# Attention scores as four 64 x 64 quarters of TensorE instead of full products with a block-diagonal key matrix

## The chip, the cores and the metric

The kernel runs on one core of a Trainium2 chip. The metric is the device time of one execution in microseconds (us), lower is better. Three runs of the kernel before took 565.74, 566.91 and 566.95 us; their median is 566.91 us. One further execution was profiled: it took 566.09 us, of which the span from the first to the last instruction is 564.3 us. The granted TensorE clock in it was 0.998 of full speed.

## The reference

For each of 8 batches, attention with pooled keys and values runs over 8 heads, and a gated MLP with mixing over the tokens follows on its result. All data are float32.

```python
def _attn_ref(q, k, v):                       # q, k, v: (8 batches, 8 heads, 576 tokens, 64)
    pool = 8
    k_p = k.reshape(B, H, 72, pool, D).mean(axis=3)       # 72 pooled keys per head
    v_p = v.reshape(B, H, 72, pool, D).mean(axis=3)
    scores = (1 / sqrt(D)) * np.matmul(q, k_p.transpose(0, 1, 3, 2))     # 576 x 72 per head
    attn = softmax(scores, axis=-1)           # max subtracted, 1e-9 added to the sum
    return np.matmul(attn, v_p)

def _moe_ref(x, w_in, w_spatial, b_spatial, w_out):       # x: (8, 576, 512)
    h = np.maximum(x @ w_in, 0)               # 512 x 1024
    u, v = halves of h
    v_n = (v - mean(v)) / sqrt(var(v) + 1e-6)
    v_s = w_spatial @ v_n + b_spatial         # 576 x 576, mixes the tokens
    return (u * v_s) @ w_out                  # 512 x 512
```

## The kernel before, in words

The work of a batch is cut into named stages. Each stage is a Python generator; every call of `next` records the instructions up to its next `yield`. Three long tables of names, `FIRST` (batch 0 with the loading of the weights), `STEP` (six times, batches 1 to 6) and `LAST` (batch 7), give the order in which the stages are stepped (`run`, line 852). Each engine executes its own instructions in exactly this recorded order, so the tables are the schedule, on TensorE (PE), VectorE (DVE), ScalarE (ACT), GpSimd (POOL) and the DMA queue of SyncE (SP). A name with a capital letter is an attention stage, which runs one batch ahead of the MLP stages in small letters; `+` and `-` move a name by a batch, and the marks `~ ^ ! %` choose a variant of a stage.

Attention stages, per batch; `g` is a pair of heads (0 to 3), `j` a pair of such pairs (0, 1):

- `K`, `V`: load keys and values, sum them in groups of 8. The plain variant does it on DVE (lines 316 to 325), one with a mark on POOL, and the `^` variant on PE, by products with the identity (`pool_pe`, line 331).
- `KT` (`att_keys_t`, line 373): transposes the pooled keys on PE and copies them from PSUM into `kp_bd`. For each pair of heads `kp_bd` holds a 128 x 144 matrix: rows 0 to 63 and columns 0 to 71 for the even head, rows 64 to 127 and columns 72 to 143 for the odd head, and zeros elsewhere, which one memset writes at the start (line 161). Copies go one head of the pair at a time.
- `Q{g}`: brings the queries of two heads into `qT`, 128 rows (2 heads x 64) by 512 tokens, and the last 64 tokens into `pt_q`.
- `S{g}` (`att_softmax`, line 524): the scores of 512 tokens for two heads. Four matmuls, one for each 128 tokens; the 128 x 128 stationary side is `qT`, the moving side the 144 columns of `kp_bd`. They go to `s_ps`, two PSUM banks of which there is one buffer only. The softmax (line 493) then reads `s_ps`: DVE takes the maximum, and either DVE subtracts it and ACT does one exponential over all (plain), or ACT does one exponential per head with the maximum as a bias (`~`), 8 of them. Only then can the next `S` write `s_ps`.
- `U{j}` (`att_softmax_l`, line 535): the same for the last 64 tokens of two pairs of heads. Two matmuls with 64 stationary columns, one into the upper and one into the lower 64 partitions of a buffer from the ring `tp` (`ps_tr`, 3 buffers), and a softmax over 2 heads.
- `T`, `Y`: bring the weights `e` of the softmax into the layout in which `A` needs them (from batch 2 on by DVE transposes and DMAs through DRAM, before that on PE). `A{half}{g}` (`att_av`, line 665): four matmuls per half and pair of heads, the product with the values.

MLP stages: `v` and `u` (products with `w_in`, lines 724, 740 and 767), `s` (product with `w_spatial`, lines 786 to 788, then gating), `o` (product with `w_out`, line 809, then the output). In these, and in `A`, every float32 product is written as three products of a high and a low part in the type float32r. The scores and the pooling are plain float32 products; each of those stands in the trace as two loads of the stationary side (LDWEIGHTS, engine PEld) and two matmuls.

The names `wv`, `wu`, `wo`, `ws` load and split weights into high and low parts. The variant `^` of such a load does the last subtraction on PE, with three products of 512 columns with the identity (lines 252 to 254), the others do it on POOL.

Of the kernel before, what the change touches and what calls it, by code (L numbers as in the profile page):

```python
# [8 lines left out]
F32 = mybir.dt.float32  # L9
# [49 lines left out]
)  # L59
STEP = (  # L60
# [9 lines left out]
)  # L70
LAST = (
# [35 lines left out]
def pooled_attention_gmlp(ctx: ExitStack, tc: tile.TileContext, q, k, v, w_in, w_sp, b_sp, w_out, out):  # L107
    nc = tc.nc
    B, H, S, D = q.shape
    P = 128  # L110
# [262 lines left out]
    def att_keys_t(kp, kr, alt=""):  # L373
# [8 lines left out]
        for e in range(2):  # L382
# [4 lines left out]
            if e == 0:  # L387
                yield
# [501 lines left out]
```

## Time and profile before

| | |
|---|---|
| median of three runs | 566.91 us (565.74 to 566.95) |
| profiled execution | 566.09 us, span 564.3 us |
| PE busy | 549.7 us (97% of the span), 3461 matmuls |
| PEld busy | 493.1 us (87%) |
| DVE busy | 370.3 us (66%) |
| ACT busy | 276.9 us (49%) |
| POOL busy | 258.4 us (46%) |
| DMA | 62.99 MB, 42.0% of the 16 engines' time on the one big queue |

Matmuls overlap in the trace: one that feeds 144 columns is listed with 286 ns, but the next starts 122 ns after it. The time that a matmul costs is therefore read from the chain of waits, where each piece is the time from the end of the piece before it to its own end, or from the distance of starts in the timeline; not from the mean duration in the table of groups.

### The profile page before, as it was taken

What the parts mean: (1) busy time and instruction counts of PE and PEld (TensorE: products, weight loads), DVE (VectorE), ACT (ScalarE), POOL (GpSimd) and SP (SyncE); (2) the same over time, 40 slices, a digit from 0 to 9 for tenths busy, and PEclk for the clock granted to TensorE, in tenths of its full rate; (3) what the DMA queues carried; (4) which work ended last, traced back from release to release, by engine and by line L of the source; (5) the groups of instructions that cost most, each with busy time, mean ns of one, the idle gap of its engine ahead of it and who ended that gap; (6) DMA issues with size and microseconds to landing.
All of it is one profiled execution on the core that took longest, in us unless ns stands there. A gap on an engine that the chain in (4) does not pass through costs nothing.

```text
span 564.3 us, 10082 instructions
## 1 busy us (share of the span) xinstructions
PE 549.7 (97%) x3461; PEld 493.1 (87%) x3461; DVE 370.3 (66%) x901; ACT 276.9 (49%) x806; POOL 258.4 (46%) x357
## 2 busy tenths in 40 slices
PE   4999999999999999999999999999999999999997
PEld 4788799987999889988998889988998889978995
DVE  3677989797857566767867577767867675535110
ACT  2697687653635535363535535363535554433221
POOL 1646565855655144651647133751547154233321
PEclk9999999999999999999999999999999999999999
DMA  8877365458204454257235364255324321100102
GB/s 241 238 231 181 76 139 102 129 140 248 70 19 113 134 108 128 69 156 164 71 98 142 127 132 117 77 148 128 93 76 121 118 76 40 43 20 0 57 2 94
DMA packets 123347, 62.99 MB, mean 112 GB/s; under 512 B 84256, under 2 KB 104736, under 8 KB 123296
## 3 DMA queue, kind: packets, MB, share of 16 engines
q1 hardware_dynamic: 123296, 62.35, 42.0%
q8 instruction: 27, 0.44, 0.3%
q14 instruction: 24, 0.20, 0.1%
HBM read 44.92 MB, written 17.40 MB: 110 GB/s over the span
## 4 chain that ended last, share of the span: by engine, by line
PE 90%; DVE 4%; ACT 3%; DMA 1%; issue 0%; SPq 0%; DVEq 0%; ACTq 0%
PE mm L809 18%; PE mm L786 17%; PE mm L767 17%; PE mm L724 15%; PE s_ps L528 5%; PE mm L331 4%; PE mm L740 3%; PE tp L672 2%; PE mm L788 1%; PE tp L675 1%; PE mm L787 1%; PE tp L673 1%; PE tp L674 1%; DMA st<-in_k 1%; PE tp L539 1%; ACT pt_rr L590 1%
## 5 line engine op out<-in xcount | busy, mean ns | idle before, releaser
L767 PE MATMUL mm<-xT,win_h 128*128 128x256 f32 (+1 forms) x512 | 104.7, 297 | 0.0
L800 POOL TENSOR_TENSOR gT<-g,gT 128x256 fp32r<-128x256 f32 x64 | 49.8, 783 | 87.6 <-ACT gT L797 87.5
L767 PEld LDWEIGHTS mm<-xT,win_h 128*128 128x128 f32 x512 | 82.2, 188 | 2.7 <-issue 1.0
L724 PE MATMUL mm<-win_h,xT 128*128 128x512 f32 x256 | 81.3, 398 | 0.7 <-ACT vv L728 0.7
L809 PE MATMUL mm<-wout_h,gT 128*128 128x512 f32 x256 | 80.7, 396 | 0.0
L786 PE MATMUL mm<-wT_h,vn_h 128*128 128x256 f32 (+1 forms) x256 | 77.2, 302 | 0.0
L786 PE MATMUL mm<-wT_l,vn_h 128*128 128x256 f32 (+1 forms) x256 | 75.8, 296 | 0.0
L786 PE MATMUL mm<-wT_h,vn_l 128*128 128x256 f32 (+1 forms) x256 | 75.7, 296 | 0.0
L767 PE MATMUL mm<-xT,win_l 128*128 128x320 f32 (+1 forms) x256 | 75.1, 293 | 0.0
L521 POOL TENSOR_TENSOR e<-e,rs 128x576 f32<-128x576 f32 (+1 forms) x48 | 44.7, 932 | 59.9 <-DVE rs L519 37.4
L791 DVE TENSOR_TENSOR g<-mm,ru 128x256 f32<-128x256 f32 (+1 forms) x64 | 28.0, 447 | 56.3 <-PE mm L788 53.3
L711 POOL TENSOR_TENSOR rstd<-rstd,neg_half 128x1 f32<-128x1 f32 (+1 forms) x40 | 23.7, 592 | 80.3 <-DVE rstd L709 80.3
L724 PEld LDWEIGHTS mm<-win_h,xT 128*128 128x128 f32 x256 | 47.1, 188 | 11.7 <-ACT vv L728 1.2
L809 PEld LDWEIGHTS mm<-wout_h,gT 128*128 128x128 f32 x256 | 47.3, 188 | 10.4 <-issue 0.2
L734 POOL TENSOR_TENSOR vn_l<-vv,vn_h 128x512 fp32r<-128x512 f32 x32 | 43.2, 1357 | 25.2 <-ACT vn_h L732 19.8
L809 PE MATMUL mm<-wout_l,gT 128*128 128x512 f32 x128 | 50.6, 395 | 0.0
L724 PE MATMUL mm<-win_l,xT 128*128 128x512 f32 x128 | 50.5, 395 | 0.0
L770 ACT ACTIVATE ru<-mm 128x320 f32<-128x320 f32 (+1 forms) x64 | 25.5, 410 | 50.2 <-PE mm L767 50.0
L797 ACT ACTIVATE gT<-g 128x256 fp32r<-128x256 f32 x64 | 26.3, 414 | 46.7 <-DVE g L791 42.1
L786 PEld LDWEIGHTS mm<-wT_h,vn_l 128*128 128x128 f32 x256 | 48.6, 190 | 0.0
L786 PEld LDWEIGHTS mm<-wT_h,vn_h 128*128 128x128 f32 x256 | 48.4, 189 | 0.2
L194 ACT ACTIVATE xT<-tp 128x256 fp32r<-128x256 f32 (+1 forms) x64 | 25.3, 408 | 47.4 <-PE tp L675 47.3
(192 smaller groups left out, 1304.6 us busy)
## 6 DMA issues: line engine op xcount, KB each, us to landing
st<-in_k SPq DMA_DIRECT2D x32, 256.0 KB, 3.3
out<-ob SPq DMA_DIRECT2D x32, 256.0 KB, 2.4
qt<-in_q SPq DMA_DIRECT2D x112, 72.0 KB, 3.2
st<-in_v SPq DMA_DIRECT2D x24, 256.0 KB, 3.4
xd<-X SPq DMA_DIRECT2D x24, 256.0 KB, 2.0
pt_l<-xd SPq DMA_DIRECT2D x24, 256.0 KB, 3.2
stw<-in_moe_w_in SPq DMA_DIRECT2D x8, 512.0 KB, 6.7
st<-in_moe_w_out SPq DMA_DIRECT2D x4, 512.0 KB, 6.6
```

The costliest lines, as they stand in the source:

```text
L194: nc.scalar.activation(hi, src, AF.Copy)
L521: nc.gpsimd.tensor_tensor(em, em, rs.unsqueeze(2).broadcast_to([m, n, SP]), op=ALU.mult)
L528: nc.tensor.matmul(s_ps[:, c // 2, (c % 2) * 2 * SP:(c % 2 + 1) * 2 * SP], lhsT=t["q", g][:, c * P:(c + 1) * P], rhs=kp_bd[:, g, :], start ...
L724: nc.tensor.matmul(a, lhsT=xT[:, i, o + c * P:o + (c + 1) * P], rhs=w[:, i, DH:], start=(i == 0 and j == 0), stop=(i == NK - 1 and j == 2))
L734: nc.gpsimd.tensor_tensor(t["vn_l"][:, c, :], vv, f32(t["vn_h"][:, c, :]), op=ALU.subtract)
L767: nc.tensor.matmul(a, lhsT=w[:, i, d * P:(d + 1) * P], rhs=xT[:, i, o + ts.start:o + ts.stop], start=(i == 0 and j == 0), stop=(i == NK - ...
L770: nc.scalar.activation(t["ru"][:, d, ts], a, AF.Relu)
L786: nc.tensor.matmul(a, lhsT=x[:, c, ds], rhs=y[:, c, ts], start=(c == 0 and j == 0), stop=False)
L791: nc.vector.tensor_tensor(g, a, t["ru"][:, d, ts], op=ALU.mult)
L797: nc.scalar.activation(dst[:, d, 0, at:at + m], g[:, o:o + m], AF.Copy)
L800: nc.gpsimd.tensor_tensor(dst[:, d, 1, at:at + m], g[:, o:o + m], f32(dst[:, d, 0, at:at + m]), op=ALU.subtract)
L809: nc.tensor.matmul(a, lhsT=src[:, i, x, at:at + m], rhs=w[:, i, :], start=(i == 0 and j == 0), stop=(i == ND - 1 and j == 2))
```

## The change

`kp_bd` is replaced by `kT`, which holds for each pair of heads a 128 x 72 matrix: the even head's keys in rows 0 to 63, the odd head's in rows 64 to 127, no zeros. Its memset is gone, and `KT` copies the main part in one instruction over all 128 partitions, then the rest in two.

`S` becomes 16 matmuls of 64 rows (one head) by 64 stationary columns (tokens) with 72 moving columns: for each 128 tokens, two halves of the tokens `i` by two heads `e`. Half `i` writes partitions 64 `i` to 64 `i` + 63, head `e` writes bank `e` of `s_ps`. `U` becomes four such matmuls instead of two, and now writes to `s_ps` and no longer to the ring `tp`. The softmax reads the two banks in the other arrangement, with the same numbers of elements.

The three tables are new. With them some stages take other variants: one more weight load takes the `^` variant (6 instead of 5), more softmaxes take `~` (17 instead of 10 of the `S`, 14 instead of 10 of the `U`), and the pooling of the values in four batches and of a few keys moves from POOL to DVE.

```diff
-    "wv1^ wv1 -K^ wv2~% -K wv2 wv2 -K -K -Q0^ -K -K -K wv1 wo0^ wv1 -Q0 -Q1^ wv1 -KT~ wo0 -Q0 -V^ -KT -Q2^ -V "
...
+    "wv0 wv0 wv0 -K^ wv3~^ -K -K wv3 wv0 -K wv3 wv0 -Q1^ wo1^! -K wv3 -K wv0 -Q0~^ wv3 -K -KT -Q0 wo1 wo1 -KT "
...
-    kp_bd = const.tile([P, NG, 2 * SP], F32, name="kp_bd")
+    kT = const.tile([P, NG, SP], F32, name="kT")
...
-    nc.gpsimd.memset(kp_bd, 0.0)
...
+        copy = nc.vector.tensor_copy if alt else nc.scalar.copy
+        copy(kT[:, :, :KM].rearrange("p (r a) s -> p r a s", r=2), main)
+        yield
         for e in range(2):
             es = slice(e * D, (e + 1) * D)
-            copy = nc.vector.tensor_copy if alt else nc.scalar.copy
-            copy(kp_bd[es, :, e * SP:e * SP + KM].rearrange("p (r a) s -> p r a s", r=2), main[es])
-            copy(kp_bd[es, :, e * SP + KM:(e + 1) * SP], rest[es, :, e, :])
-            if e == 0:
-                yield
+            copy(kT[es, :, KM:], rest[es, :, e, :])
...
         s_ps = ps.tile([P, 2, 512], F32, name="s_ps", tag="s")
+
         for c in range(NC):
-            nc.tensor.matmul(s_ps[:, c // 2, (c % 2) * 2 * SP:(c % 2 + 1) * 2 * SP],
-                             lhsT=t["q", g][:, c * P:(c + 1) * P], rhs=kp_bd[:, g, :], start=True, stop=True)
+            for i in range(2):
+                for e in range(2):
+                    es, at = slice(e * D, (e + 1) * D), c * P + i * TL
+                    nc.tensor.matmul(s_ps[i * TL:(i + 1) * TL, e, c * SP:(c + 1) * SP],
+                                     lhsT=t["q", g][es, at:at + TL], rhs=kT[es, g, :], start=True, stop=True)
         yield
-        em = yield from softmax(s_ps[:, :, :4 * SP].rearrange("p a (h s) -> p a h s", h=4), P, 8, alt)
+        em = yield from softmax(s_ps[:, :, :4 * SP].rearrange("p e (c s) -> p e c s", s=SP), P, 8, alt)
...
-        sl = ps_tr()
+        sl = ps.tile([P, 2, 512], F32, name="s_ps", tag="s")
         for i in range(2):
-            nc.tensor.matmul(sl[i * TL:(i + 1) * TL, :2 * SP], lhsT=t["ql", j][:, i, :], rhs=kp_bd[:, 2 * j + i, :],
-                             start=True, stop=True)
+            for e in range(2):
+                es = slice(e * D, (e + 1) * D)
+                nc.tensor.matmul(sl[i * TL:(i + 1) * TL, e, :SP], lhsT=t["ql", j][es, i, :],
+                                 rhs=kT[es, 2 * j + i, :], start=True, stop=True)
         yield
-        em = yield from softmax(sl[:, :2 * SP].rearrange("p (a h s) -> p a h s", a=1, h=2), P, 2, alt)
+        em = yield from softmax(sl[:, :, :SP].unsqueeze(2), P, 2, alt)
```

The first place at which the new tables matter is PE in the steady part (batches 2 to 7). Before, a `U` stands among the products of `A` (L672 to L675) and writes to the ring `tp`. Lines of the changed kernel are 25 to 29 lower, so that `U` (L539) is L514 there, `S` (L528) is L501, `s` (L786 to L788) is L761 to L763, and `o` (L809) is L784. In the order before:

```order
L809 MATMUL mm<-wout_l,gT 128x512
L672 MATMUL tp<-pt_h,vm_h 128x256
L673 MATMUL tp<-pt_h,vm_l 128x256
L674 MATMUL tp<-pt_l,vm_h 128x256
L675 MATMUL tp<-pt_rr,vr 128x256
L539 MATMUL tp<-kp_bd,pt_q 64x144 x2
L672 MATMUL tp<-pt_h,vm_h 128x256
```

In the order of the change, one `U` and the `S` that follows it, with the 14 products of one `s` between them:

```order
L650 MATMUL tp<-pt_rr,vr 128x320
L514 MATMUL s_ps<-kT,pt_q 64x72 x4
L761 MATMUL mm<-wT_h,vn_h 128x320
...
L762 MATMUL mm<-wT_h,vt 128x320
L763 MATMUL mm<-wT_l,vb 128x320
L501 MATMUL s_ps<-kT,qT 64x72 x16
L784 MATMUL mm<-wout_h,gT 128x512 x2
```

The `U` and the `S` now write the same single buffer `s_ps`, one stage apart. In all other places of the steady part an `S` or a `U` stands alone between full-size products, before and after. On DVE, the maximum of this `U` (L467, L498 before) stands in the order of the change behind a subtraction of the softmax of an `S`, two transposes of `Y` and a product of the gating, which waits for a buffer that POOL frees:

```order
L475 TENSOR_TENSOR e<-s_ps,mx 128x2x4x72
L623 STREAM_TRANSPOSE XL<-e 128x128
L625 STREAM_TRANSPOSE XLR<-pt_p 64x32
L766 TENSOR_TENSOR g<-mm,ru 128x256
L467 TENSOR_REDUCE mx<-s_ps 128x2
L469 TENSOR_SCALAR mx<-mx 128x2
```

The second place is PE at the start. Before, the transposes of queries follow the pooling of the keys, and the first weight split comes behind the transposes of the keys:

```order
L331 MATMUL mm<-st_r,ident 64x64 x8
L474 MATMUL tp<-ident,qt 128x128 x4
L475 MATMUL tp<-ident,qt 128x64
L377 MATMUL tp<-ident,kp 128x128 x2
L378 MATMUL tp<-ident,kr 128x64
L252 MATMUL mm<-x,ident 128x512
L253 MATMUL mm<-win_h,ident_m 128x512
L254 MATMUL mm<-z,ident_p 128x512
```

In the order of the change the first weight split (L223 to L225) stands directly behind the pooling, and the transposes follow:

```order
L302 MATMUL mm<-st_r,ident 64x64 x8
L223 MATMUL mm<-x,ident 128x512
L224 MATMUL mm<-win_h,ident_m 128x512
L225 MATMUL mm<-z,ident_p 128x512
L348 MATMUL tp<-ident,kp 128x128 x2
L349 MATMUL tp<-ident,kr 128x64
L444 MATMUL tp<-ident,qt 128x128 x4
L445 MATMUL tp<-ident,qt 128x64
```

What moved: the split of a weight now covers the time in which ACT copies the pooled keys out of PSUM, which before the first transposes of queries covered.

More of the change, by code (lines that the diff above doesn't have):

```diff
@@ L493, in softmax @@
     def softmax(sv, m, n, alt):
-        a = sv.shape[1]
         mx = ring("mx", 2, [P, 8], F32, "mx")[:m, :n]
-        mv = mx.rearrange("p (a h) -> p a h", a=a)
+        mv = mx.rearrange("p (c e) -> p e c", e=2)
         nc.vector.tensor_reduce(mv, sv, axis=AX.X, op=ALU.max)
@@ L502, in softmax @@
         em = ring("e", 3, [P, 8, SP], F32, "e")[:m, :n, :]
-        ev = em.rearrange("p (a h) s -> p a h s", a=a)
+        ev = em.rearrange("p (c e) s -> p e c s", e=2)
         sm = ring("sm", 2, [P, 8], F32, "sm")[:m, :n]
@@ L513, in softmax @@
             for h in range(n):
-                nc.scalar.activation(em[:, h, :], sv[:, h * a // n, h % (n // a), :],
+                nc.scalar.activation(em[:, h, :], sv[:, h % 2, h // 2, :],
                                      AF.Exp, bias=mx[:, h:h + 1], scale=QK, accum_out=sm[:, h:h + 1])
```

105 rows, old and new, of tables (FIRST, LAST, STEP) are left out of this document.

## The prediction

> **What bounds the kernel now.** I read the page's first part, then the windows over three steady stretches, then what PE waits for.
>
> ```profile
> PE 549.7 (97%) x3461; PEld 493.1 (87%) x3461; DVE 370.3 (66%) x901; ACT 276.9 (49%) x806; POOL 258.4 (46%) x357
> ```
>
> ```profile
> core 0: us, PE busy (x) PEld busy (x) DVE busy (x) ACT busy (x) POOL busy (x), PEclk, DMA share, GB/s
> 0.00:20.00 20.00, 12.16 (x75) 10.26 (x77) 8.32 (x23) 6.60 (x13) 4.91 (x13) 1.00 0.77 218
> 132.00:194.00 62.00, 62.00 (x390) 56.29 (x389) 40.96 (x103) 29.47 (x86) 31.10 (x44) 1.00 0.37 101
> 382.00:447.00 65.00, 65.00 (x404) 58.75 (x403) 48.13 (x120) 31.59 (x92) 28.80 (x43) 1.00 0.39 101
> ```
>
> ```profile
> PE mm L331 <- DMA st<-in_k: 7.8, 1, 7.8
> PE mm L724 <- ACT vv L728: 0.7, 1, 0.7
> PE s_ps L528 <- DVE qT L484: 0.7, 1, 0.7
> PE s_ps L528 <- DVE e L506: 0.6, 1, 0.6
> PE tp L672 <- DVE pt_rr L592: 0.4, 1, 0.4
> PE s_ps L528 <- ACT e L514: 0.2, 1, 0.2
> ```
>
> In a step of one batch PE is busy 62.00 of 62.00 us, while DVE fills 41 to 48, ACT 29 to 32 and POOL 29 to 31. Over the whole span PE waits 7.8 us for the first keys and 2.6 us in five further places. The clock is 1.00, so no throttle hides anything. Hence the time is the sum of what PE's products cost, and the question is what a score group costs between its neighbours, before and after.
>
> **What S and U cost now.** From the chain of waits, where a piece is the time it adds:
>
> ```profile
> 289.13 0.98 PE s_ps L528 x8
> ...
> 308.69 0.12 PE tp L675
> 308.81 0.40 PE tp L539 x4
> 309.20 0.31 PE tp L672
> 309.51 0.12 PE tp L673
> ...
> 41.37 1.07 PE mm L331 x16
> 42.45 0.32 PE tp L672
> 42.76 0.12 PE tp L673
> ```
>
> A full-array S is 8 passes (four products, two passes each) in 0.98 us, 0.122 per pass of 144 columns. A U is 4 passes of 64 stationary columns: it adds 0.40 us, and the first full-size product behind it takes 0.31 instead of 0.12, so it costs 0.40 + 0.19 = 0.59 us. The chain of waits thus shows a price that is paid once for going from the full array to a part of it and back.
>
> How large is it? A U's four passes start at once in pairs, one in the upper and one in the lower column half:
>
> ```profile
> 288.97 1.14 PE L528 MATMUL s_ps<-kp_bd,qT 128*128 128x144 f32 x8
> ...
> 308.73 0.20 PEld L539 LDWEIGHTS tp<-kp_bd,pt_q 128*64 128x64 f32 x4
> 308.74 0.47 PE L539 MATMUL tp<-kp_bd,pt_q 128*64 128x144 f32 x4
> ```
>
> ```profile
> L539 PEld LDWEIGHTS tp<-kp_bd,pt_q x64: 132/134/136, 19.9 to 449.6; 128*64 128x64 f32 x64
> ```
>
> One load of U lasts 0.134 us, yet all four together span 0.20, and the four matmuls, each of median 0.312, span 0.47. Four passes in a row, 0.122 apart, would span 0.312 + 3 × 0.122 = 0.68; two rounds of two span 0.312 + 0.16 = 0.47. So column halves run side by side, U is two rounds, and the round trip costs 0.59 − 2 × 0.122 = 0.346 us. The pooling group on 64 x 64 tiles (16 passes on one and the same quarter) costs 1.07 + 0.20 = 1.27 us; less 0.346 that is 0.92 / 16 = 0.058 per pass of 64 columns.
>
> The Trainium skill has a rule that speaks against this change: "TensorEngine Tiling (Array Packing)", section Key Properties, says that a change of tiling mode drains the array. The trace agrees, with those 0.346 us; by the rule, all 32 S now pay it, 11 us of the 31 that S takes, and this is in the sum below.
>
> **S and U after.** An S becomes 16 products, 32 passes of 72 columns. No row shows four quarters running at once; two column halves are shown above, and two row halves here (two products that read 64 rows each, one from each half, side by side in 0.27 us, where one lasts 272 ns in the groups):
>
> ```profile
> 24.67 0.27 PE L631 MATMUL tp<-ident,e 64*128 64x64 f32 x2
> ...
> L631 PE MATMUL tp<-ident,e 64*128 64x64 f32 x8 | 1.1, 272 | 0.0
> ```
>
> I take it that both hold together, since the order in the code goes through the four quarters one after the other. Then S is 8 rounds. A round of 72 columns costs between half of the 0.122 of 144 columns, 0.061, and 0.058 × 72/64 = 0.065; I take 0.063. S after = 0.346 + 8 × 0.063 = 0.85 us, against 0.98. U after = 0.346 + 2 × 0.063 = 0.47, against 0.59.
>
> - 32 S gain 0.13 each: 4.2 us (0.114 to 0.146: 3.6 to 4.7).
> - 16 U gain 2 × (0.122 − 0.063) = 0.12 each: 1.9 us.
> - Together 6.1 us (5.5 to 6.6).
>
> In the order of the change, as before, nearly every S and U stands alone among full-size products, so no round trip is shared.
>
> **What PE gets in addition.** One more weight load takes the variant that splits on PE:
>
> ```profile
> 16.66 1.06 PE mm L252 x2
> 17.72 0.23 PE mm L253
> 17.95 0.23 PE mm L254
> ```
>
> That is 1.52 us. It stands directly behind the pooling of the keys. Before, PE is through with that pooling at 15.3 us (below), while DVE takes up the first weight piece at 10.63 us and the next at 12.89, so the inputs of the first split are there about 2 us ahead of PE, and I expect no wait. Net on PE: 6.1 − 1.5 = 4.6 us less (4.0 to 5.1).
>
> ```profile
> 10.63 0.43 DVE L226 TENSOR_SCALAR x<-x 128x512 uint32<-128x512 uint32 x1 [7.21 <-ACT x L221]
> 12.89 0.42 DVE L226 TENSOR_SCALAR x<-x 128x512 uint32<-128x512 uint32 x1
> ...
> 15.30 0.59 PE tp L474 x4
> ```
>
> **What I cost at nothing.** Seven more S take the `~` softmax and the pooling of four batches of values goes from POOL to DVE.
>
> ```profile
> 97.11 2.54 ACT e L514 x16
> ...
> L508 ACT ACTIVATE e<-e 128x576 f32<-128x576 f32 x22 | 14.8, 674 | 2.3 <-DVE e L506 2.3
> L506 DVE TENSOR_TENSOR e<-s_ps,mx 128x576 f32<-128x576 f32 x22 | 16.5, 750 | 0.8
> L510 DVE TENSOR_REDUCE sm<-e 128x8 f32<-128x576 f32 x22 | 16.3, 742 | 8.0 <-ACT e L508 8.0
> L320 POOL TENSOR_TENSOR st<-st 128x512 f32<-128x512 f32 x10 | 12.9, 1294 | 0.0
> L320 DVE TENSOR_TENSOR st<-st 128x512 f32<-128x512 f32 x14 | 9.8, 700 | 3.3 <-DMA st<-in_k 3.3
> ```
>
> A `~` adds 2.54 − 0.67 = 1.9 us to ACT and takes 0.75 + 0.74 = 1.5 from DVE. With one or two more in a batch, ACT goes from 31 to at most 35 of 62 us. A pooled piece of values costs DVE 0.70 where it cost POOL 1.29; a batch's worth is 3 to 4 us, about what the `~` take away. DVE stays below 50 of 62, and PE's cover is whole. If it were not, the price is in rival B. The missing memset and the fewer copies of keys lie beside PE's work and count nothing. The five small waits of 2.6 us in all may shift, vanish or grow; the one way in which they vanish reaches 7.2 us gained, and I leave them.
>
> **Sum.** Against the profiled execution: 566.09 − 4.6 = 561.5 us (span 559.7). Against the median of 566.91, 0.8 higher, it is 562.3. I say 562.0, and 561.0 to 562.9 from the bounds of the terms alone; with 2.6 us of waits gained or as much lost, 558.4 to 565.5. A difference of 0.2%, 1.1 us, is the least that counts as one here.
>
> **Rivals.**
>
> *A: only two quarters run at a time.* The trace shows pairs in columns and pairs in rows, never four. If a round holds two, S has 16 rounds: 0.346 + 16 × 0.063 = 1.35 us, 0.37 more than now, 32 × 0.37 = 12 us; U has four rounds, 0.60, no change; with the 1.5 us of the split the time is 566.5 + 13.5 = 580 us. It decides as soon as S needs more than 10 rounds ((0.98 − 0.346) / 0.063). With none together S would be 2.3 us and the time about 612. For it: no row excludes it. Against it: both pairings work on the same loads and matmuls, and the order of the products suits it.
>
> The Trainium skill, "TensorE: Matmul & The Clock Gate", Part 3, "The mechanism", lets a load pass running matmuls only where the row groups differ, by which the two column halves would go one after the other and A would hold. The trace disagrees for two of them, with four loads in 0.20 us, and has no row for four quarters.
>
> *B: the score buffer.* U now writes `s_ps`, of which there is one, and in each of six steps an S follows a U after 14 products of `s`.
>
> ```profile
> 288.98 0.15 PE mm L788
> ...
> 309.25 0.31 DVE L498 TENSOR_REDUCE mx<-tp 128x2 f32<-128x144 f32 x1 [0.55 <-PE tp L539]
> ...
> 270.53 0.47 PE L539 MATMUL tp<-kp_bd,pt_q 128*64 128x144 f32 x4
> 273.47 0.26 DVE L498 TENSOR_REDUCE mx<-tp 128x2 f32<-128x144 f32 x1
> ```
>
> At 0.147 us each, the 14 take 2.06, so S is due 0.47 + 2.06 = 2.5 us after the start of U. With a free DVE the maximum starts 0.51 us after it (308.74 to 309.25), and with 0.31, a scaling of 0.2 and two exponentials of 0.3 the buffer is free after about 1.8 us: no wait. But that maximum stands on DVE behind a subtraction (0.75), two transposes and a gating product that waits for POOL. If it comes 2.94 us after U, as at 270.53, the buffer is free after 4.2 us and PE waits 1.7 us, six times: 10 us, and the whole is 562 + 10 = 572. From 0.8 us of wait a step on it eats the gain. What stands behind that S on PE are the products of `o`, so the time is lost in full. Against it: before, DVE is late by that much in some places only, and PE's other waits on `s_ps` sum up to 1.5 us.
>
> *C: no change.* The round of 72 columns is not shorter than the one of 144, or the new order at the start, where PE is idle for 8 of 20 us, waits for a split or a query by 2 to 4 us more. With S at 0.346 + 8 × 0.08 = 0.99 the gain is gone but for 1.3 us of U, less than the split: 566 to 567.
>
> **How the numbers follow.** The forecast has 0.62 (558.4 to 565.5), A 0.13 (580 or more), B 0.12 (566 to 572), C 0.13 (565 to 568). The time is that of the forecast, 562.0. The range leaves out A and the upper end of B, some 0.17 in all, and takes in the rest: 558.0 to 570.0. Faster by over 0.2% are the forecast and a tenth of B and of C, together 0.65; within 0.2% are most of C and some of B, 0.13; slower are A, the rest of B and of C, 0.22.
>
> **What would show it.** In the changed profile: S (L501) as a piece of 0.60 to 0.70 in the chain of waits and a first product behind it of 0.31; its 32 passes spanning about 0.75 in the timeline, in rounds of four starts; PE at 62 of 62 or less per step, no new row of waits for `s_ps` above 1 us in sum. A piece of 1.1 or more for S means A; a row "s_ps <- ACT" or "<- DVE" of several us means B; a longer wait before 20 us means C. The forecast is wrong if the round trip for four quarters costs more than 0.48, or a round more than 0.08 us, since either takes the gain of S.

## The result

Four runs of the changed kernel took 557.05 us (556.75 to 557.56), the kernel before on the same chip 566.33 (565.66 to 566.95): a ratio of 0.984, 95% interval 0.982 to 0.985. That is 9.3 us faster where 4.6 were forecast, and below the range that was given (558.0 to 570.0).

The page of the changed kernel, first part, then two of the windows and the waits of PE:

```profile
PE 539.7 (97%) x4297; PEld 479.1 (86%) x4297; DVE 374.7 (68%) x930; ACT 291.6 (53%) x916; POOL 229.4 (41%) x316
```

```profile
132.00:194.00 62.00, 62.00 (x523) 55.30 (x525) 39.71 (x100) 31.45 (x102) 29.98 (x42) 1.00 0.43 118
382.00:447.00 65.00, 65.00 (x524) 58.17 (x522) 46.98 (x119) 36.03 (x123) 21.48 (x33) 1.00 0.43 114
```

```profile
PE mm L302 <- DMA st<-in_k: 7.9, 2, 6.6
PE s_ps L514 <- ACT e L483: 1.1, 1, 1.1
PE s_ps L501 <- DVE e L475: 1.0, 1, 1.0
PE s_ps L514 <- DVE e L475: 0.7, 1, 0.7
PE mm L742 <- DVE wT_l L167: 0.4, 1, 0.4
PE tp L552 <- DVE sm L486: 0.3, 1, 0.3
```

PE still fills 62.00 of 62.00 us per step, while DVE, ACT and POOL are below 48 of 62 to 65. The waits for the score buffer, 2.8 us, all fall in the first 34 us; behind them PE waits 0.3 us at 46 us and 0.4 us at 84 us, and then no more. So the kernel is bound as before, and what changed is what PE's products cost. The chain of waits of the changed kernel, an `S` among products of 256 columns and a `U` among products of 320:

```profile
288.74 0.11 PE mm L763
288.85 0.66 PE s_ps L501 x32
289.51 0.32 PE tp L647
289.83 0.11 PE tp L648
...
295.39 0.15 PE tp L650
295.54 0.29 PE s_ps L514 x8
295.83 1.95 PE mm L761 x12
```

`S` costs 0.66 + (0.32 − 0.12) = 0.86 us, where 0.98 stood before and 0.85 was forecast. `U` costs 0.29, and the 12 products behind it 1.95 instead of 12 × 0.147 = 1.76, together 0.48; forecast 0.47, before 0.59. The timeline of an `S` (start, duration, engine, number), and the rows of its line over the whole kernel (least, median and largest ns, first and last start), show the four quarters at work together:

```profile
288.78 0.73 PE L501 MATMUL s_ps<-kT,qT 64*64 64x72 f32 x32
...
288.78 0.58 PEld L501 LDWEIGHTS s_ps<-kT,qT 64*64 64x64 f32 x32
```

```profile
L501 PEld LDWEIGHTS s_ps<-kT,qT x1024: 129/133/133, 18.3 to 456.8; 64*64 64x64 f32 x171
L501 PE MATMUL s_ps<-kT,qT x1024: 222/223/274, 18.3 to 456.9; 64*64 64x72 f32 x171
```

32 loads of 0.133 us each are through in 0.58 us, and 32 matmuls of 0.223 in 0.73. By their starts in the trace they come in eight rounds of four: the four of a round start within 0.02 us, the second round 0.113 us behind the first, and each later one 0.062 to 0.063 us behind the one before it. The terms that the prediction worked out for `S` and `U` are therefore right, and another one must be missing. It is found in work that the change does not touch. The chain of before (first two rows) and of after (last two), stretches of 512-column products of the same batch:

```profile
325.99 1.87 PE mm L740 x8
327.86 5.60 PE mm L724 x24
```

```profile
324.08 1.83 PE mm L715 x8
325.91 2.75 PE mm L699 x12
```

Eight products take 1.83 us instead of 1.87, and one product 2.75 / 12 = 0.229 instead of 5.60 / 24 = 0.233. From the distances of the starts in the trace, over the 810 or so of these products that follow one of their own kind, the mean falls from 233.1 to 229.9 ns, and that of the products of 256 columns in `u` and `s` from 118.7 to 117.1; those of 320 columns hardly move (146.8 and 146.6). Neither their shapes nor their number have changed, and the granted clock is the same.

Two measures are used from here on. The **pitch** is this distance between the starts of two products. The **main part** runs from the first product with `w_in` to the start of the last product of the kernel:

```profile
L724 PE MATMUL mm<-win_h,xT x256: 389/394/504, 55.7 to 511.0; 128*128 128x512 f32 x128
L809 PE MATMUL mm<-wout_l,gT x128: 390/394/398, 115.7 to 559.8; 128*128 128x512 f32 x128
```

```profile
L699 PE MATMUL mm<-win_h,xT x256: 387/392/505, 55.6 to 498.2; 128*128 128x512 f32 x128
L784 PE MATMUL mm<-wout_l,gT x128: 388/394/398, 114.9 to 550.8; 128*128 128x512 f32 x128
```

It was 504.1 us before and is 495.2 now, 8.9 less. The start-up ahead of it took 55.7 and 55.6 us; it hangs on the first loads and moves by more than a microsecond between executions of the same program order (below), so that differences of a few microseconds are best read from the main part.

### The profile page after: what moved, and what is told of

Its sections match the earlier page's. It is cut to its first block, busy times and chain, and to the rows that moved or that the text cites. A ratio compares the mean times of both kernels' runs of the same rounds, so it can differ in the third digit from the quotient of the medians.

```text
span 554.9 us, 11870 instructions
## 1 busy us (share of the span) xinstructions
PE 539.7 (97%) x4297; PEld 479.1 (86%) x4297; DVE 374.7 (68%) x930; ACT 291.6 (53%) x916; POOL 229.4 (41%) x316
## 4 chain that ended last, share of the span: by engine, by line
PE 89%; DVE 5%; ACT 2%; DMA 1%; issue 1%; POOL 1%; SPq 1%; DVEq 0%; ACTq 0%
PE mm L761 19%; PE mm L784 18%; PE mm L742 17%; PE mm L699 16%; PE s_ps L501 4%; PE mm L715 2%; PE tp L647 2%; PE mm L762 2%; PE mm L763 2%; PE tp L650 1%; PE tp L649 1%; PE tp L648 1%; DMA st<-in_k 1%; PE mm L302 1%; PE s_ps L514 1%
## 5 line engine op out<-in xcount | busy, mean ns | idle before, releaser
L742 PE MATMUL mm<-xT,win_h 128*128 128x320 f32 (+1 forms) x512 | 104.1, 298 | 0.4 <-DVE wT_l L167 0.4
L775 POOL TENSOR_TENSOR gT<-g,gT 128x256 fp32r<-128x256 f32 x64 | 47.1, 745 | 125.4 <-ACT gT L772 125.3
L784 PE MATMUL mm<-wout_h,gT 128*128 128x512 f32 x256 | 80.4, 395 | 0.0
L761 PE MATMUL mm<-wT_h,vn_h 128*128 128x256 f32 (+1 forms) x256 | 76.5, 299 | 0.0
L761 PE MATMUL mm<-wT_l,vn_h 128*128 128x256 f32 (+1 forms) x256 | 75.5, 295 | 0.0
L761 PE MATMUL mm<-wT_h,vn_l 128*128 128x256 f32 (+1 forms) x256 | 75.4, 294 | 0.0
L742 PE MATMUL mm<-xT,win_l 128*128 128x256 f32 (+1 forms) x256 | 75.1, 293 | 0.0
L483 ACT ACTIVATE e<-s_ps,mx 128x72 f32<-128x72 f32 x164 | 50.1, 332 | 20.3 <-DVE mx L469 18.7
L784 PEld LDWEIGHTS mm<-wout_h,gT 128*128 128x128 f32 x256 | 46.9, 188 | 9.9
L167 DVE TENSOR_TENSOR xT<-tp,xT 128x320 fp32r<-128x320 f32 (+1 forms) x64 | 28.5, 447 | 33.2 <-ACT xT L165 32.8
L709 POOL TENSOR_TENSOR vn_l<-vv,vn_h 128x512 fp32r<-128x512 f32 x32 | 41.6, 1316 | 21.9 <-ACT vn_h L707 21.8
L784 PE MATMUL mm<-wout_l,gT 128*128 128x512 f32 x128 | 50.4, 394 | 0.0
L761 PEld LDWEIGHTS mm<-wT_h,vn_h 128*128 128x128 f32 x256 | 48.1, 188 | 1.0 <-DVE wT_l L285 0.3
L761 PEld LDWEIGHTS mm<-wT_h,vn_l 128*128 128x128 f32 x256 | 48.2, 188 | 0.1
L761 PEld LDWEIGHTS mm<-wT_l,vn_h 128*128 128x128 f32 x256 | 48.1, 188 | 0.0
```

The costliest lines, as they stand in the source:

```text
L167: nc.vector.tensor_tensor(lo, src, f32(hi), op=ALU.subtract)
L483: nc.scalar.activation(em[:, h, :], sv[:, h % 2, h // 2, :], AF.Exp, bias=mx[:, h:h + 1], scale=QK, accum_out=sm[:, h:h + 1])
L709: nc.gpsimd.tensor_tensor(t["vn_l"][:, c, :], vv, f32(t["vn_h"][:, c, :]), op=ALU.subtract)
L742: nc.tensor.matmul(a, lhsT=w[:, i, d * P:(d + 1) * P], rhs=xT[:, i, o + ts.start:o + ts.stop], start=(i == 0 and j == 0), stop=(i == NK - ...
L761: nc.tensor.matmul(a, lhsT=x[:, c, ds], rhs=y[:, c, ts], start=(c == 0 and j == 0), stop=False)
L775: nc.gpsimd.tensor_tensor(dst[:, d, 1, at:at + m], g[:, o:o + m], f32(dst[:, d, 0, at:at + m]), op=ALU.subtract)
```

## The experiments

Times are medians, and ratios are to runs of the kernel before on the same chip (565.67 us beside the tables, the quarters for `S` alone, `U` behind `S` and the row halves; 566.45 beside the four runs on the place up to the map; 566.54 beside the two single executions, the map and the turned loops; 566.07 beside the last two).

**Is it the tables or the quarters?** The first run takes the new tables alone, with the old products.

```diff
 (kernel before, with FIRST, STEP and LAST of the change)
-        sl = ps_tr()
+        sl = ps.tile([P, 2, 512], F32, name="s_ps", tag="s")[:, 0]
```

> Only the new tables: the kernel before with the three tables of the change, S and U as full products with the block-diagonal keys (U writes the buffer s_ps, as the tables need it). Theory Q (the quarters did it): S and U cost 0.12 and 0.10 us more each again (3.9 + 1.6 us), and the products of 512 columns, which follow each other every 229 ns in most of the changed kernel, go back to the 233.4 ns of before (3.7 us over all products): 557.05 + 9.2 = 566.3. Theory T (the tables did it): the 229 ns stay, and only S and U cost more: 557.05 + 5.5 = 562.6.

565.99 us, ratio 1.001 (0.999 to 1.003). The pitch of 512 columns is 233.1 ns on the mean, as before; two rows of its chain of waits:

```profile
329.74 1.87 PE mm L711 x8
331.60 2.80 PE mm L695 x12
```

The main part is 503.7 us, 0.4 less than before. So the tables by themselves bring nothing that counts, and 229 ns is not theirs. That is what theory Q said, but the next run took it down as well. It puts the quarters into the kernel before, for `S` alone:

```diff
-            nc.tensor.matmul(s_ps[:, c // 2, (c % 2) * 2 * SP:(c % 2 + 1) * 2 * SP],
-                             lhsT=t["q", g][:, c * P:(c + 1) * P], rhs=kp_bd[:, g, :], start=True, stop=True)
+            for i in range(2):
+                for e in range(2):
+                    es, at = slice(e * D, (e + 1) * D), c * P + i * TL
+                    nc.tensor.matmul(s_ps[i * TL:(i + 1) * TL, e, c * SP:(c + 1) * SP],
+                                     lhsT=t["q", g][es, at:at + TL], rhs=kp_bd[es, g, e * SP:(e + 1) * SP],
+                                     start=True, stop=True)
```

> Only the new products, and those only in S: the kernel before, its tables, its block-diagonal keys and its U, with S as 16 products on quarters that read the non-zero blocks. Theory Q: S costs 0.12 us less each, 3.9 us, and the products of 512 columns behind an S run at 229 ns, so up to 3.7 us more: 566.3 - 3.9 - (1.5 to 3.7) = 558.7 to 560.9. Theory T: 566.3 - 3.9 = 562.4, and 233.4 ns in nearly all stretches.

562.17 us, ratio 0.994 (0.991 to 0.996), main part 501.2. `S` costs 0.66 in the chain, as in the change, and 27 `S` of the main part at 0.12, 3.2 us, cover the 2.9 us by which it is shorter. But in its chain the stretch right behind an `S` shows the old pitch (5.80 holds also the 0.20 of the way back to the full array):

```profile
314.93 0.66 PE s_ps L530 x32
315.59 5.80 PE mm L727 x24
321.39 1.87 PE mm L743 x8
323.25 5.60 PE mm L727 x24
```

Quarters in front of a stretch do not make it faster, so theory Q is wrong. What the kernels with 233 ns have in common, and those with 229 do not, is the block-diagonal matrix: 2304 bytes per partition instead of the 1152 of `kT`. Tiles lie in SBUF in the order in which the code makes them. The weights `win_h`, `wout_h` and `wT_h` come ahead of the keys and stay; `xT`, `gT` and all others come behind and move by 1152 bytes, 4.5 times 256. By the addresses of the program, the moving sides `win_h` and `wout_h` start at byte 160 of a 256-byte line; the stationary sides `xT` and `gT` start at byte 224 before and at byte 96 after. One stationary side moves the other way: `gt`, which holds the last 64 tokens of two batches for `o`, starts at byte 96 before and at 224 after.

**Is it the place in SBUF?** The same one line in both kernels, 128 unused bytes per partition behind the keys:

```diff
     kT = const.tile([P, NG, SP], F32, name="kT")          (before: kp_bd)
+    const.tile([P, 32], F32, name="pad")
```

> The changed kernel with 128 unused bytes per partition behind the tile of the keys, nothing else. The block-diagonal keys took 1152 bytes per partition more, so the change moves every tile that lies behind them in SBUF, with them the stationary sides xT and gT, by 4.5 times 256 bytes, while the moving sides win_h and wout_h, which lie ahead, stay. Theory P (placement): the distance between two products of 512 columns follows from where the stationary side starts within 256 bytes, 229 ns where it starts at byte 96 and 233.4 where it starts at 224; the pad moves xT and gT to 224, the distance goes back to 233.4 ns and the time to 557.0 + 3.7 = 560.7. Theory C (something else in the new code decides): 229 ns and 557.0 stay.

> The kernel before with the same 128 unused bytes behind its keys, nothing else. Theory P: xT and gT start at byte 96, the 512-column products follow each other every 229 ns and the time falls by 3.7 us, to 562. Theory C: no change, 565.7.

The changed kernel goes up to 559.88 us, ratio 0.988 (0.985 to 0.991), its main part from 495.2 to 498.8. The kernel before goes down to 561.97, ratio 0.992 (0.989 to 0.995), its main part from 504.1 to 500.5. The chains, first of the changed kernel with the pad, then of the kernel before with it:

```profile
324.85 1.87 PE mm L716 x8
326.71 2.80 PE mm L700 x12
```

```profile
324.90 1.83 PE mm L741 x8
326.74 5.49 PE mm L725 x24
```

Each kernel takes the pitch of the other (means 233.0 and 229.6 ns). Theory P holds in both directions, at 3.5 to 3.6 us of the main part. This is the missing term: a smaller tile has moved others to a better place.

The products with `gt` confirm it inside each kernel. They have the same shape and the same moving side as those with `gT`, but the opposite start, and in all four traces their pitch is near 229 to 230 ns where that of `gT` is near 233, and the other way round (mean pitch in ns, start in brackets):

```
                            gT             gt
before                 233.4 (224)    229.1 (96)
after                  230.1 (96)     233.7 (224)
after, 128 bytes       233.2 (224)    230.1 (96)
before, 128 bytes      229.5 (96)     233.3 (224)
```

**Which places are good?** Two further placements were tried in the kernel that has `U` behind `S` (the next question); then a run that measures the pitch by itself.

> The kernel with U behind S, with 192 unused bytes behind the keys: xT and gT start at byte 32 of 256, the weights stay at 160, a distance of 128. If the start of the stationary side alone decides by the half of 256 bytes in which it lies (96 fast, 224 slow), 32 is fast: 553. If the distance between both sides decides, 128 is a new case between 64 (slow) and 192 (fast).

556.12 us, ratio 0.981 (0.979 to 0.984): 2.7 us more than without the pad. 512 columns are 232.5 ns apart. So start 32 is slow although it lies in the same half of a line as 96, and the start of the stationary side alone does not decide by halves; the byte difference between the two sides, 128 here, remains as a candidate.

> The kernel with U behind S, with 96 unused bytes ahead of the weights and 64 behind the keys, so that the weights (win_h, wout_h, wT_h), xT and gT all start at a multiple of 256 bytes. If only the distance between the two sides within 256 bytes counts (192 where the products are 229 ns apart, 64 where 233.4), 0 is a third case and open. If an access that does not cross a 256-byte line is cheaper, 512 columns come below 229 ns: down to 220 would be 880 x 9 ns = 8 us less, 545. Otherwise 553 to 557.

552.33 us, ratio 0.975 (0.972 to 0.978), 512 columns at 228.5 ns, 256 columns of `u` at 119.7 instead of 115.3. The hoped for 220 ns does not come; the gain on the wide products is nearly given back on the narrow ones, in which the roles of `xT` and `win_h` are swapped.

```diff
+    for w, n in ((512, 12), (256, 16), (320, 16)):
+        for so in range(0, 64, 8):              # start of the stationary side, in floats
+            for mo in range(0, 64, 16):         # start of the moving side
+                probe(w, n, so, mo)             # n products of w columns, xT[.., so + ..] by win_h[.., mo:mo + w]
```

> The changed kernel with 96 further stretches of products behind its end, which nobody reads: 12 products of 512 columns, 16 of 256 and 16 of 320, with the stationary side starting 0, 32, ... 224 bytes and the moving side 0, 64, 128 or 192 bytes behind the place of before (byte 96 and byte 160 of 256). Theory P: the distance within a stretch depends on these two starts alone; 512 columns take 229 ns at (96, 160) and 233.4 at (224, 160), 228 to 233 elsewhere. If only the distance of both starts modulo 256 counts, all pairs with the same distance agree within 1 ns; if a pair has one of 220 or less, it is worth placing for. Rival: no pattern by the starts, and the distance follows from what ran ahead. The time of the whole is 557 + about 330 us.

789.25 us in one execution, 232 more than the change by itself; the 330 were a wrong estimate. Three of its 96 stretches in the chain of waits, with the stationary side at 96, 160 and 224 and the moving side at 160:

```profile
551.39 2.81 PE mm L846 x12
...
574.55 2.78 PE mm L846 x12
...
597.69 2.85 PE mm L846 x12
```

The first products of a stretch are slower, so the table below takes the mean over the last 6 (512 columns) or 8 (256). Rows are the start of the stationary side in a 256-byte line, columns that of the moving side; all in ns.

```
512 columns              256 columns
       160   224    32    96       160   224    32    96
  96  229.0 233.2 233.3 230.8     113.4 118.1 113.2 119.2
 160  226.7 228.8 233.3 233.3     120.0 117.8 119.2 113.4
 224  233.3 228.3 228.8 232.7     113.2 119.2 117.8 118.1
  32  232.3 233.3 226.7 228.8     118.1 113.4 120.0 117.9
 others (0, 64, 128, 192):
      233.0 to 234.8              116.6 to 120.2
```

For 512 columns the byte difference (stationary minus moving, modulo 256) parts these rows into two groups, 0 and 192 below 231 ns and 64 and 128 above 232: 0 gives 226.7 to 230.8, 192 gives 228.8 to 229.0, 128 gives 232.3 to 233.3 and 64 gives 233.3. For 256 columns 64 is best, 113.2 to 113.4, and 0 worst, 119.2 to 120.0; one field does not fit and stays unexplained: (96, 160) has 113.4, where the other three with a difference of 192 have 117.8 to 117.9. Products of 320 columns are at 146.4 to 146.8 in all 32 places. The same products, in the same program, thus differ by 3% and by 6% with nothing but the place. The claim that equal differences agree within 1 ns does not hold for 0.

**What does a change to quarters and back cost?** In 11 places the four products of `U` were put directly behind the 16 of `S`:

```diff
+        if (t["b"], g) == (2, 2) or t["b"] >= 3 and g % 2 == 0:
+            ...
+                    nc.tensor.matmul(s_ps[i * TL:(i + 1) * TL, e, NC * SP:(NC + 1) * SP], lhsT=t["ql", j][es, i, :],
+                                     rhs=kT[es, 2 * j + i, :], start=True, stop=True)
+            t["sl", j] = s_ps
```

> The changed kernel, with the four products of U directly behind those of S, in columns 288 to 359 of the same two banks, in 11 of the 16 places (U1 of batch 2, both U of batches 3 to 7). If the cost of a U is the round trip of 0.346 us and two rounds of 0.063, each such U now costs 0.13 instead of 0.47 to 0.49: 11 x 0.36 = 3.9 us less, 553.1. Rival: each group pays on its own even side by side, or the score buffer, held until the softmax of U is through, makes the next S wait: 557 or more.

553.39 us, ratio 0.978 (0.976 to 0.980), main part 491.8, 3.4 less than the change. The chain of waits (the window cuts the `S` off at its front):

```profile
255.00 0.39 PE s_ps L501 x26
255.38 0.12 PE s_ps L508 x8
255.51 5.70 PE mm L709 x24
```

Behind an `S` a `U` costs 0.12 us, two rounds of 0.063, and no round trip; 11 × 0.36 = 3.9 were expected. The 0.346 us that the prediction read from the trace of before is a price per visit to the quarters, not per product.

**Would two row halves do as well?** `S` as 8 products of 64 rows by 128 columns:

```diff
-            for i in range(2):
-                for e in range(2):
-                    es, at = slice(e * D, (e + 1) * D), c * P + i * TL
-                    nc.tensor.matmul(s_ps[i * TL:(i + 1) * TL, e, c * SP:(c + 1) * SP],
-                                     lhsT=t["q", g][es, at:at + TL], rhs=kT[es, g, :], start=True, stop=True)
+            for e in range(2):
+                es = slice(e * D, (e + 1) * D)
+                nc.tensor.matmul(s_ps[:, e, c * SP:(c + 1) * SP],
+                                 lhsT=t["q", g][es, c * P:(c + 1) * P], rhs=kT[es, g, :], start=True, stop=True)
```

> The changed kernel with S as 8 products of 64 rows by 128 columns instead of 16 of 64 by 64: two row halves side by side. If a round of two row halves costs the 0.063 us of a round of four quarters, S stays at 0.85 us and the time at 557. Rival: the loads of 128 columns, or the switch, cost more than those of quarters: a pass of 0.112 (as 128 x 128 transposes) gives S 0.346 + 8 x 0.112 = 1.24, and 557 + 12 = 569; if the halves do not run together, 16 x 0.063 + 0.346 = 1.35 and 573.

567.78 us, ratio 1.005 (1.003 to 1.007): the rival was right. The chain of waits, and the row of the line's loads:

```profile
307.06 1.04 PE s_ps L500 x16
```

```profile
L500 PEld LDWEIGHTS s_ps<-kT,qT x512: 182/188/242, 19.7 to 470.2; 64*128 64x128 f32 x171
```

`S` costs 1.04 + 0.20 = 1.24 us, as worked out from 0.112 per round. A load of 128 columns takes 0.188 us where one of 64 takes 0.133, and the eight rounds are 0.105 to 0.112 us apart, about as the 128 x 128 products of the pooling, which follow each other every 0.112 us. Both versions of `S` have eight rounds, so what the row halves lose against the quarters is the time of a round, 0.112 against 0.063, with a stationary side of 128 columns against 64.

**Does the order among the quarters matter?** The loops were turned round, so that one quarter gets its four products in a row:

```diff
-        for c in range(NC):
-            for i in range(2):
-                for e in range(2):
+        for i in range(2):
+            for e in range(2):
+                for c in range(NC):
```

> The changed kernel with the 16 products of an S in another order: the four 128-token groups of one quarter one after the other, then the next quarter, where the change goes through the four quarters in turn. If PE starts products only in the order of the program, so that quarters run together only because neighbours in the order stand on different quarters, most of an S is serial: 32 passes of 0.058 to 0.063 less the few that overlap at the three borders, 1.8 to 2.2 us instead of 0.66 to 0.85, and the time 557 + 32 x (0.95 to 1.35) = 587 to 600. If PE picks products for free quarters ahead of the order, S stays at 0.85 and the time at 557.

583.75 us in one execution, and 1.56 us for each `S` in the chain:

```profile
286.98 1.56 PE s_ps L501 x32
```

It is 0.90 us more per `S`, 29 over all; the time rose by 27. Most of the products now run one by one, 0.057 to 0.063 us apart, which is also the distance of the rounds of four in the change; with 0.20 for the way back an `S` costs 1.76 us, a little less than the 1.8 to 2.2 that were expected, since more products overlap than those at the three borders. In this order PE did not find the free quarters ahead: they help only where neighbours in the program stand on different ones.

**The map put to use.** 64 unused bytes behind `xT` (and in the kernel before also the 128 behind its keys) bring `gT` to byte 160, `vn_h`, `vn_l` and `pt_h` to 96:

```diff
     xT = const.tile([P, NK, LO + S], F32R, name="xT")
+    const.tile([P, 16], F32, name="pad")
```

> The kernel with U behind S, with 64 unused bytes behind xT, so that gT starts at byte 160 of 256, vn_h and vn_l at 96 and pt_h at 96, while xT, the weights and vm_h stay. By the map of the placements: products with wout and gT (both starts 160) fall from 230 to 226.7 ns, 384 of them, 1.2 us; the 256-column products of s (wT 160, vn 96 in place of 32) from 118.6 to 113.3 ns, 384 of them, 2.0 us; the 256-column products of A (pt_h 96, vm_h 32) from 118 to 113.5, 128 of them in groups of four, 0 to 0.6 us. Together 2.8 to 3.8 us: 553.4 becomes 549.6 to 550.6. Rival: what the map shows for long even stretches does not hold in the short, mixed ones of the kernel, 552 to 553.4.

> The kernel before, its tables and its products, with two unused strips, 128 bytes behind its keys and 64 behind xT. By the map all starts then stand as in the run with U behind S and the 64 bytes: 4.0 us less from xT and gT at 229 ns as measured with the first strip alone, and 2.8 to 3.8 more from gT, vn and pt_h: 566.4 becomes 558.6 to 559.6. If the map does not carry over to another kernel, 562 as with the first strip alone.

552.62 us, ratio 0.976 (0.974 to 0.979), main part 490.7, only 1.1 less than without the strip; and 561.41, ratio 0.992 (0.990 to 0.994), main part 498.5, 2.0 less than with the first strip alone. The products of `o` with `gT` fell as the map says in part, from 230.2 to 228.1 and from 229.5 to 227.8 ns (226.7 expected), the 256-column products of `s` from 118.6 to 117.6 and 116.8 (113.3 expected). They stand in stretches of 14 that alternate with 320 columns and with products of other tiles, and there the place may bring less than in the long even stretches of the map. But the 113.3 for `s` was read from the one field that does not fit, (96, 160); the other fields with its difference of 192 have 117.8, close to what came. The runs do not show how much of the map a mixed stretch keeps, and the medians of whole runs hardly tell the difference. The versions with `U` behind `S` are the fastest ones found, at 552.3 to 553.4 us, except the one with 192 unused bytes.

## Why the prediction was wrong

The main part is 8.9 us shorter. The runs divide it: tables 0.4 (504.1 to 503.7), place in SBUF 3.5 to 3.6, products the rest, 4.9. The last term is also measured: the run with the new tables and the old products (503.7) and the changed kernel with 128 unused bytes (498.8) have the same tables and the same starts, and differ by 4.9.

- **The bound**: right. PE is as full as before, and the time follows what its products cost.
- **S and U**: right, each within 0.01 us (0.86 and 0.48 against 0.85 and 0.47), with the round of four at 0.063. 27 `S` and 14 `U` of the main part at 0.12 and 0.11 make 4.8 us, and the runs leave 4.9 for them.
- **The split**: its price was right. One of the two that the main part now holds, where it held one before, in the chain of the changed kernel:

```profile
59.51 1.06 PE mm L223 x2
60.56 0.23 PE mm L224
60.80 0.23 PE mm L225
```

- **The small waits**: left out of the sum, with up to 2.6 us to gain. In the main part, three waits of 1.6 us became one of 0.4, which about makes up for the split; the table run, in which the split and the new order are contained, shows 0.4 us in all. The waits were 1.2 us of the miss. The start-up was to gain 0.9 us from five `S` and two `U` and gained 0.1; the time behind the start of the last product fell by 0.4.
- **The step that failed** is the sentence that the missing memset and the fewer copies of the keys "lie beside PE's work and count nothing". It saw the key matrix as work alone. Its size set where `xT` and `gT` lie, and so the pitch of products that the change does not touch. The two pads measured it at 3.5 to 3.6 us, the larger part of the miss of 4.7: 880 products of 512 columns at 3.2 ns each are 2.8 us, and 832 of 256 columns at 1.5 ns another 1.2, together a little more than the pads show. The trace of before held a hint that I did not read, two pieces of one line in its chain of waits:

```profile
309.87 5.61 PE mm L809 x24
...
316.65 2.75 PE mm L809 x12
```

  The first 24 products have `gT` as stationary side and stand 0.234 apart, the last 12 have `gt` and stand 0.229 apart: the same shape at two prices in one kernel, at the starts 224 and 96.
- **Rival A** is refuted: eight rounds, not sixteen. An `S` in which the quarters mostly do not run together does exist, but it takes another order of the loops, and it cost 27 us.
- **Rival B** is refuted for the steps: the `S` behind a `U` waits nowhere in the main part; the 14 products cover the softmax. In the start-up the single buffer does cost something: the waits for `s_ps` there rose from 0.6 to 2.8 us, more than the 1 us of new waits that the forecast allowed. That may be why the start-up gained so little; no run separates it.
- **Rival C** is refuted: the round of 72 columns costs 0.063, not 0.08, and the start-up is as long as before.

The rule of the Trainium skill on the change of tiling mode ("TensorEngine Tiling (Array Packing)", section Key Properties) was borne out by the `U` behind `S`, which paid no second round trip; that the 0.346 us are a drain is not shown. The rule that loads pass running matmuls only where the row groups differ ("TensorE: Matmul & The Clock Gate", Part 3, "The mechanism") does not agree with the run of the change: 32 loads of 0.133 us on two row halves and two column halves were through in 0.58 us, and two at a time would need 16 × 0.133 = 2.1 us.

## What to carry to other kernels

Small products gain from quarters of the array only if neighbours in the program stand on different quarters, and each visit has a price (0.35 us here), so put the small products of several stages side by side before splitting them finer. When a change alters the size of a tile, list which operands behind it move; if the pitch of untouched products differs between two traces, compare the starts of both operands before looking for a cause in the schedule, and undo the shift with a strip of unused bytes to see what the change itself is worth.

## What was not expected

- The pitch of products of the same shape depends on where their two operands start in 256 bytes: 226.7 to 234.8 ns for 512 columns, 113.2 to 120.2 for 256, no effect on 320 (146.4 to 146.8). Why is not shown.
- Within a stretch the pitch repeats in a fixed pattern, such as 226, 229, 232 ns or 231, 236, and a stretch needs some products to settle into it.
- A round with a stationary side of 64 columns takes 0.063 us whether one quarter or four take part; one with 128 columns on two row halves takes 0.11.
- The start-up differs between executions: the first product of the same program, but for unused bytes, started at 6.6 and 6.7 us in the changed kernel and at 7.8 and 6.5 in the kernel before, and the main part began at 55.6 and 54.5, and 55.7 and 56.4 us.
